# VectorE turns x in squares of 32 instead of TensorE, and the experts' scores become three products of rounded halves in 64x128 tiles

## Chip, core and metric

One core of one Trainium2 chip. The time is the device time of one execution in microseconds; for a kernel it is the median of its runs. Nothing here crosses to another core.

## What is computed

Block-sparse attention over 4 sequences of 768 tokens (8 heads of 64), whose output x, 512 wide, goes into a mixture of 4 attention experts. Cut to what matters:

```python
# attention: blocks of 32; a query block sees its neighbours, the first and last block and 3 drawn ones;
# the first and the last query block see everything
scores = np.where(mask, scale * q @ k.T, -1e9); x = softmax(scores) @ v          # x: (4, 768, 512)
logits = x @ w_gate                                   # the two best of 4 experts per token, weights w
for e in range(4):
    q, k, v = x @ wq[e], x @ wk[e], x @ wv[e]         # 64 wide
    a = softmax(np.where(causal, -1e9, 0.125 * q @ k.T))
    out += w_of_e * (a @ v @ wo[e])                   # only where e was chosen
```

The expert weights wq and wk are 64 times larger than the others, so the experts' scores need nearly full 32-bit precision.

## The kernel before, in words

**Attention.** Each sequence has 11 units of two query blocks and one "ends" unit ("g") for the first and last block. A unit gathers its keys into a tile `ks` (GpSimd copies, L620, and L300 or L298 on any of three engines), its values into `vs` (DMAs, L633 to L642), and then runs: scores on PE (mask rows L659, products L668, in 64x32 tiles), row maxima on DVE (L675, L678), exponentials on ACT (L686), four PE transposes (L697) into a PSUM bank, a copy out to `pt` (L292 on ACT or L294 on DVE), and the product with the values on PE (L714, 128x32 tiles). The ends unit does the same over all 768 keys (L760, L773, L779, L789, L802).

**x.** The product lies in a PSUM bank as queries by features. DVE multiplies it by the reciprocal row sums into an SBUF tile `x` (L731), PE transposes `x` by two 128x128 transposes into another bank (L557), ACT writes the rounded upper half `xh` (L578, L580) and DVE the remainder `xl` (L585, L587). These two halves, features by tokens, are what the experts' projections read.

**Experts.** When a chunk of tokens is done (3 tiles of 128 tokens; 4 and then 2 in the last sequence), PE projects V and the gate (L832) and Q and K for two pairs of experts (L852), each as three products of halves (`xh*wh`, `xl*wh`, `xh*wl`) in a 32-bit form that the matmul rounds. Q and K are copied out once, unrounded, to `qk` (L292 on ACT or L294 on DVE). For every row tile r of 128 queries and each pair p of experts ("a score block", 48 in all, over 128(r+1) keys): the causal mask (L934) and the scores (L943) in 64x32 tiles as full 32-bit products, which the trace shows as two MATMUL records for each instruction; maxima (L956, DVE), exponentials (L961, ACT), gate weight over row sum (L966 to L968, DVE), scaling (L975, GpSimd or DVE), transposes (L991, PE), copies to `pte` (L292, L294), the product with V (L1012, PE), halves `oh` and `ol` (L1022 ACT, L1027 DVE), output projection (L1036, PE), a copy to `y` and a store.

**Order.** All this is recorded as operations with an engine (or a choice), a duration and dependences. A table of characters, `ORDER`, found by a search outside, says in which sequence each engine gets its instructions; `replay` assigns buffers and PSUM banks from small pools along it. The engines run in their order and wait by semaphores. Changes between PE tile shapes (128x128, 128x32, 64x32) happen where neighbours in the order differ. At the start, SP, ACT and GpSimd issue the loads: K (`kt`), Q (`qt`), values, and the weights, which arrive in the still unused `qk` and `vb` tiles and are split into halves (L440, L449).

Of the kernel before, what the change touches and what calls it, by code (L numbers as in the profile page):

```python
# [25 lines left out]
ORDER = (
    "#$#&#,#2#)$W$N$P$S#/#5#;%U$]$Y$k%N$;$A%V$>$D$`#c$o&s%P$l%Y%]&3&u$u'##?#u$r&5%`%c%f$x%l%o%i&>%x%r&9)O*4'&(k&A${%/"
    "%#%,$d$J%u%2%{&;')%&'8'5#D%5',&D';(l&#%*%>&&#g%8%;&y'Y&P&G&S%A'?#x&{&V$G'V&J']'G&Y&M'`(u&]'c&`'/'r'u(x&c'3'f&)'i"
    "%D({'A'D&,)/),)#(p&f&/'J(,$#'x'l)2&i%G(r#B#H,<#o%J(/)T*5)P(D'{#8,>$)(2)Y*>(G(J#i)5)>)])`)&)))c&l)l)o(##J(')8);(Y"
    ")f*s*A#r'o)i)V$g*#)A*9'M'P$&'S&o#{)r*D)u*;)D(;)G*P)J)x){*&(N#l+X(P(5#]#`#P*S()*)*G*V*u+Y#S-f(S*,(8*/#V(?(V*J(A#M"  # L30
    '(]#Y*Z-l(`+c(c(f+f+i*M+#+&.&+)-i.)+8+,+l+u+x-{.#-`*x*{02-o+5.8-d/5-r5W.;/80;/>05+//;+2-u/A.,.>+;,G-x.A.D08*]*`/D'
    '+G*c.G,{-#,J/K/H$3,B,D+].K+o0>.2,M+>$,5J9i5P5H5N6G6J5c.5,]/M$5,Y,P.0.N*f.P+r/Q.T+A+D.`.i+J.l.c0`,S+M+{0i.f.o.s0c'
    '.v-&-)+`*i,V,`,#*l,c+P-,,f.V,i+S0A*o.x,l-/0l0f.{1;.Y/],o-27l0G->,&-A-5,)/S-8-D0D.]0o1>,,/f,/0s/`-P-H5j5T5f0v0P,r'
    ",2/i-;/c,5,u-J/#-M,8,x6S-S-V-Y/&1A1D-]0x$81V1#/l/V/)6V7-0{1G1'/Y1K5o0J0M6Y6i/o/s$/1M0S6f1P1]1`;l/u9l5l5r5u5x1iFP"
    '7/7o6N735Z1Z1S6)6]6&1o2x1m3&1x2{3)1r1{3#1c1u6,1f2#3,2&68;o322)3//,1)2A/y//6/2D2J780V/{2G7;2M0Y0#0&5{6l1,7x1/0]7>'
    '7A7M6o2,226$9e2/7J356`386c62652P262W7{6;3P9f:N2S755]7r/27u6P5a3S3Y8#8&8/823A123V3;16:I:J853?893D3]424;3G4>45483J'
    '2`2Y0)4A0,:P0/3`2^2c4f4D3M4H4o4r9o4i282;2>9r4l2f8)7D4P9u9x4J6r6u2i8-3g8A2l3d4M:&4S8;7H6x6{4V9{4Y:)3i3o3m:#3r7#3u'
    '8>8S:87&3y7)8D8l8V:S8o3{4u<P4x4|8Q:,4#:/4&7]:V2o7P8G:28Y4]:58J8M:;:Y6>:i:]:f5#7T2r:x5&8]8c5/5)4`4c8`7V7Y8g526A6D'
    '5,7`9&9>9)7c558i2u={187f9A:l:`9,9J:>9D:p:c9G9N:r:u:A:{958r8x;#8v<S;2FcFM:D9P9/8{;,;/;&;)>f7i93999;9#>`9S9V9Y9]9`'
    ';x>d;{=v>i>Y>^>{>u>l>o?#58<#</<&<2;8>y?2?;?5;;?&<)>r?8?>?A<-;>;A;J=5=8=x?,;M?/<5<85;?E?H?J?*?Y?c?f?]AYA]?`<]A,;P'  # L40
    '?iAc?MA`AfA/;]4)A2;S>#A5A8;r;5<`;D;GFBFJ;u4->&FGFE?lGAGD?p;V;Y?r>)<c<o<r<u<f<i@/?v;`=&<y<V<Y=A@8<m>,>8>/>;?P<;@;'
    '@2=D@5>>;c5>>2?SAi?VA;AB=G=J;f;i<A=SA><><{=V=#AD<DAG<G=Y=f=)>6=;4/=>>B5A=,AJ<J=/J^GMANF_=]<MGP>D>G=M=P>JB5?xAP=`'
    '=cJ`H&H)KGFSAmF`GSAo?{B8=2@#>M@>ASGV>P@&=i=lG`@BGc=oFi>S@VFf>VAVAx=rGfFl@YBP@`@]@c@fFoFrArBVFVGGGJAvA{@)G#@mBSF{'
    'Gi@EBY5D@GBA@KCr@M@j@o@P@sBDC{@SCuB;B#@uB>KACxBiH2D#BGBrBlH5BuGYBJBMBoD&G]B&BxG2C$B]FuB`HfHiD)B{FyBcC,BgH8H;HGG&'
    "@xHDC;G)@{HrC>CAB)CDCGC&A#HuN/H-G,G/C)C/CJCQCNA'JdG5HxH{I)DJI,D/KJD,CSDMDSC2DPDVD3CWGlCYD;DYD^E,HVA)H/GoC]GrC5C`"
    'E5C8GuD>I/E/D5B,CcCfI3E8E2GxE;E`EcEiB/D`D8HJH>HADAHPHMEfKDE>HSEA@,HmHoJfDiEDFZEHDDElDoDcEJEMG{CiIKI;DgDmEoDrH#HY'
    "EPESJiClDGJlIMJoJrDuIfEVIiL&ErIPEvK#J{ISKMK2KPI#ExEYI&E]IVH]F)F#E{IZKSH`HcF'I5I8DxKVKYIlI]KcK`KfF,F/I>D{IaIcIoF2"
    'K&JuF5K*KiJxI{J#LfK]KlKoJ&IAE#IrJ8L,L/CoIDIuJ;K,K/IxJME&JDJ>JAIGK5J)LiG8JHG;LrJ/KrJ,J3KuN2L)MQE)B2F8LuLxKxK{JJJ5'
    'K8OYJPNqNrL#G>L2K;F;K>JSLlLoJVL{M,O`JYL5OdM#N6OSOoOWMLMMWEW?L8LGOsL;M&M)O]OfM/M3OuW<WB]AN8MVMYLDOiOxP,P5P8Q)P/Q,'
    'P2Q/LJP&L>P)LAN;OlP;P?Q2M5M8Q5M]PBN>M`NAMiLMQ8M;PDO{M>P$PHR&MlQ;Q>NMNPNDPSR)PVP]R,QAMAP`PYQPNGR/NJQSLV]DWMMDQDR2'  # L50
    'McLPLSPJMgN{NSWGMSPMN`PcWKPfNuNxLYPPMGPjQYWWPlMoNVO#MsNYPoQVPrN]RSO&PuWYW^W`PxQ]O5O)O2R]R5NcL]M{Q`P{Q#L`R`RVR<Qf'
    'O8ODO,NfMuMxX{F>Y&XAO;WcR8NiRYX;X>N#LcQdN&N)O/NlWfN,Q&S/XDO>S2WiWuQGOARcOGY#XGOJWlQJRDS5OMYaOPRfRiWxXJXMW{XY]|SV'
    'X$SYR>S;RlS9X]XPRpS>RBRGSAS]WoWsXlSDY,Y/SGS`T5T8QMX,RrSJY2T;Y5QiRuT>TATDY>YASPSTRxRJSMQlRMR{ScTlS#RPX`SfSlSoSiS&'
    'TGYcTJTMXdToTrTPX&QoQrX)SrTuTxSuSyQuS*S{XST#X/TSXV[WTVYlYoYrZ#V&V/V2YuT&T*QxV)T{U$YDV,TYT,Q{Z&T/T]YHY)R#YfYiUDV5'
    "U'T`V<U)V8UMT2U,S,Z)Z,VJUPUG]=]>WQV>U/VDXfXiU5U2UJU8VBVHZ5VNXoY8Y;[YUSVYV]V`Vc[cUYWT[fVfU;UVU]YxUcXrYP[i[u[lViY|"
# [1037 lines left out]
```

## Time and profile before

| | |
|---|---|
| Runs | 486.59, 488.38, 489.38 us; median 488.38 |
| Profiled execution | 486.6 us, of which the span of the profile is 484.8 us; mean granted clock 0.996 |
| ACT busy | 287.6 us |
| POOL busy | 171.9 us |
| Moved by DMA | 60.87 MB, mean 126 GB/s |

The profile covers one execution. A page of it gives busy time by engine, the span in 40 slices, the chain of waits (the work that ended last, followed back from the end) and groups of instructions; the timeline lists PE's instructions by start. Matmuls are pipelined: a record's length includes the way through the array, so what a matmul costs is the distance from its start to the next start. "PE bk L852" is PE work of line 852 that writes PSUM (`bk`).

### The profile page before, as it was taken

The page shows a single profiled execution, that of the slowest core. Times are in us where ns is not written, and L with a number is a line of the kernel's source. Part 1 is how long each engine was busy: PE and PEld are TensorE (multiplying, and loading weights), DVE is VectorE, ACT ScalarE, POOL GpSimd, SP SyncE. Part 2 cuts the span into 40 slices and gives each one's busy share as a digit, 9 for nine tenths or more (in the row PEclk, how much of TensorE's full clock was granted, in tenths as well). Part 3 has the DMA queues.
Part 4 walks back from the last instruction along what each step waited for, and adds up shares of the span by engine and source line. Part 5 has one row for each costly group of instructions (what it writes and reads, how often), then busy time and mean ns, then how long its engine had stood idle before and what let it go on. Part 6 is the DMA issues. An engine that isn't in the chain of part 4 may idle for free.

```text
span 484.8 us, 24898 instructions
## 1 busy us (share of the span) xinstructions
PE 458.8 (95%) x10068; PEld 364.3 (75%) x10068; DVE 340.5 (70%) x951; ACT 287.6 (59%) x907; POOL 171.9 (35%) x464
## 2 busy tenths in 40 slices
PE   3877998999999999999999999999999999999996
...
GB/s 231 232 273 218 145 223 84 125 74 114 168 67 178 90 99 214 132 164 56 103 151 145 101 188 242 131 163 40 3 70 229 157 84 144 22 25 3 23 24 88
DMA packets 37756, 60.87 MB, mean 126 GB/s; under 512 B 9817, under 2 KB 16074, under 8 KB 37642
## 3 DMA queue, kind: packets, MB, share of 16 engines
...
## 4 chain that ended last, share of the span: by engine, by line
PE 86%; DMA 4%; issue 3%; DVE 3%; SPq 3%; ACT 2%; DVEq 0%; ACTq 0%
PE bk L852 14%; PE bk L714 8%; PE bk L943 8%; PE bk L1012 8%; PE bk L697 8%; PE bk L991 8%; PE bk L832 7%; PE bk L668 7%; PE bk L1036 6%; PE bk L557 2%; PE bk L802 2%; PE bk L789 2%; PE bk L760 2%; DMA vs<-in_v_dram 2%; SPq L642 2%
## 5 line engine op out<-in xcount | busy, mean ns | idle before, releaser
L686 ACT ACTIVATE p<-bk,mx 128x256 f32<-128x256 f32 x176 | 82.3, 483 | 26.5 <-DVE mx L678 21.8
L975 POOL TENSOR_SCALAR pe<-pe,mxe 128x640 f32<-128x640 f32 (+5 forms) x49 | 35.4, 728 | 147.8 <-DVE mxe L968 93.8
L961 ACT ACTIVATE pe<-bk,mxe 128x640 f32<-128x640 f32 (+5 forms) x96 | 60.7, 636 | 40.9 <-DVE mxe L956 40.3
L620 POOL COPY ks<-kt 128x128 f32 x264 | 65.0, 296 | 17.0 <-PE bk L668 16.9
L956 DVE TENSOR_REDUCE mxe<-bk 128x1 f32<-128x384 f32 (+5 forms) x96 | 56.2, 616 | 19.3 <-PE bk L943 18.8
L675 DVE TENSOR_REDUCE mx<-bk 128x4 f32<-128x1024 f32 x44 | 53.5, 1217 | 14.8 <-PE bk L668 14.8
L714 PE MATMUL bk<-vs,pt 128*32 128x64 f32 x2816 | 51.8, 221 | 4.1 <-DMA vs<-in_v_dram 2.5
L292 ACT ACTIVATE pte<-bk 128x512 f32<-128x512 f32 (+2 forms) x73 | 39.3, 552 | 26.7 <-PE bk L991 18.6
L714 PEld LDWEIGHTS bk<-vs,pt 128*32 128x32 f32 x2816 | 43.7, 110 | 14.7 <-issue 6.6
L668 PE MATMUL bk<-ks,qt 64*32 64x256 f32 x1408 | 50.3, 387 | 3.5 <-DMA qt<-in_qT_dram 3.5
L697 PE MATMUL bk<-ident,p 128*128 128x128 f32 x352 | 52.8, 279 | 0.4 <-DVE pte L294 0.3
L300 POOL COPY ks<-kt 128x256 f32<-128x256 f32 x40 | 15.0, 407 | 98.8 <-PE bk L668 85.7
L991 PE MATMUL bk<-ident,pe 128*128 128x128 f32 x336 | 49.9, 278 | 0.0
L943 PE MATMUL bk<-qk 64*32 64x512 f32 (+3 forms) x1024 | 47.2, 447 | 0.6 <-issue 0.6
L697 PEld LDWEIGHTS bk<-ident,p 128*128 128x128 f32 x352 | 39.3, 141 | 10.8 <-issue 3.1
L852 PE MATMUL bk<-xh,wqkh 128*128 128x384 f32 (+2 forms) x128 | 45.2, 353 | 0.0
L294 DVE COPY pte<-bk 128x512 f32<-128x512 f32 (+2 forms) x55 | 31.0, 575 | 19.9 <-PE bk L991 12.3
L1012 PE MATMUL bk<-pte,vb 128*32 128x128 f32 x1344 | 44.4, 275 | 0.5 <-issue 0.3
L991 PEld LDWEIGHTS bk<-ident,pe 128*128 128x128 f32 x336 | 37.6, 141 | 9.1 <-issue 3.3
L852 PE MATMUL bk<-xh,wqkl 128*128 128x384 f32 (+2 forms) x128 | 43.0, 336 | 0.0
L852 PE MATMUL bk<-xl,wqkh 128*128 128x384 f32 (+2 forms) x128 | 43.0, 336 | 0.0
L1012 PEld LDWEIGHTS bk<-pte,vb 128*32 128x32 f32 x1344 | 35.0, 110 | 8.6 <-issue 5.7
...
## 6 DMA issues: line engine op xcount, KB each, us to landing
...
```

The source lines that it names most:

```text
L620: pol.tensor_copy(K[:, :, k0:k0 + 32], KT[:, :, bass.ds(rv[c * NR + k] * 32, 32)])
L668: pe.matmul(Sb[32 * c:32 * c + 32, e, j * 256:(j + 1) * 256], QT[m, 2 * hh + j, q0:q0 + 32], KS[ks.i][m, 2 * hh + j, 128 * blk:128 * blk + ...
L675: vec.tensor_reduce(MX[mx.i][:, 0].rearrange("p (j e) -> p e j", e=2), BK[:, bs.i:bs.i + 2].rearrange("p e (j k) -> p e j k", j=2), AX.X, ...
L686: acte.activation(P[p.i][:, e, j], BK[:, bs.i + e, j * 256:(j + 1) * 256], AF.Exp, scale=scale, bias=MX[mx.i][:, 0, i:i + 1], accum_out=MX ...
L697: pe.transpose(BK[:, bt.i, c:c + 128], P[p.i][:, e, j, h * 128:(h + 1) * 128], ident)
L714: pe.matmul(BK[32 * c:32 * c + 32, bo.i, (2 * j + e) * 64:(2 * j + e) * 64 + 64], PT[pt.i][:, j, h, 32 * c:32 * c + 32], VS[vs.i][:, blk + ...
L852: pe.matmul(BK[:, bk.i, 0:n1 - n0], w[:, k, m0:m0 + 128], a[:, k, n0:n1], start=n_ == 0, stop=n_ == 3 * KT_ - 1)
L943: pe.matmul(BK[32 * c:32 * c + 32, banks[e].i + c0 // 512, 0:cw], QE[p][m, q0:q0 + 32], KE[p][m, c0:c0 + cw], start=c0 + cw < nk, stop=Tru ...
L956: vec.tensor_reduce(MXE[mx.i][:, 0, e:e + 1], bank(), AX.X, op=ALU.max, negate=True)
L961: acte.activation(PE_[pb.i][:, e, 0:nk], bank(), AF.Exp, bias=MXE[mx.i][:, 0, e:e + 1], accum_out=MXE[mx.i][:, 1, e:e + 1])
L991: pe.transpose(BK[:, bt.i, i * 128:(i + 1) * 128], PE_[pb.i][:, e, t * 128:(t + 1) * 128], ident)
L1012: pe.matmul(BK[32 * c:32 * c + 32, bo.i, 0:128], VB[:, t, c0:c0 + 32], PTE[ptb.i][:, e, t * 128:(t + 1) * 128], start=t == 0, stop=t == r, ...
```

## The change

Seven parts.

1. **x turned by VectorE.** The heads are laid out so that a 32-wide strip of the bank holds one pair of heads. DVE writes the scaled product back into the other half of the same PSUM bank and turns it in 32x32 squares into the first half; the two PE transposes and the tile `x` are gone. Features then lie in another order on the partitions, and the weights are loaded to match (`(p k)` instead of `(h p j)`).
2. **Experts' scores from halves.** Q and K are split at the copy out: ACT writes a rounded upper half and DVE the remainder (`QHL`, two buffers, and `KHL`). The score block is then three products, each with two instructions in 64x128 tiles, one per expert of the pair. The mask is four instructions of 64 columns instead of eight.
3. **Weights at the start.** wq and wk arrive in two of the three `pe` buffers, as packets of 1024 bytes instead of 512, one DMA each; wv is one DMA instead of two; all of them go through SP (`loadq`).
4. Unit masks are built for two blocks in one tile (`dup`), one mask instruction per 32-query strip as before (two for units at the edge).
5. The last sequence's chunks are 3 and 3 tiles, as the others' were.
6. Pools: `vs` 4 instead of 5 buffers.
7. The recording's numbers and the table `ORDER` are new.

The diff, cut to its core:

```diff
-MODEL = dict(... loadq="POOL|SP", wrel=18.0)
+MODEL = dict(... loadq="SP", xt=340, dma0=2000, wrel=18.0)
 ORDER = (
-    "#$#&#,#2#)$W$N$P$S#/#5#;%U$]$Y$k%N$;$A%V$>$D$`#c$o&s%P$l%Y%]&3&u$u'##?#u$r&5%`%c%f$x%l%o%i&>%x%r&9)O*4'&(k&A${%/"
+    '#,#2#&##$K$M$D$G$S#/#A#>$V$2#5&$$g#)$8#;$i%B#J$Y$b$5%H%J$;$c$l$o%D&&%M%P#D&`&c(P&/&2$r$u%#%&$x${$P&*%)%-%/%2%5(S'
...
-    pools = dict(ks=3, vs=5, p=2, pt=4, mx=4, x=2, pe=3, pte=2, mxe=4, oh=2, y=2)
+    pools = dict(qe=2, ks=3, vs=4, p=2, pt=4, mx=4, pe=3, pte=2, mxe=4, oh=2, y=2)
-    QK = fixed("qk", [128, 2 * EP, S])
+    KHL = fixed("khl", [128, 2, EP, S], F32R)
+    QHL = [fixed(f"qhl{i}", [128, 2, S // 2], F32R) for i in range(pools["qe"])]
...
+        wb = [buf("pe", 12 + 0.2 * i) for i in range(2)]
+            def fn(q, i=i):
+                q.dma_start(XWQ(i).rearrange("p e k d -> p e (k d)"), (wq, wk)[i].rearrange("e (p k) d -> p e (k d)", k=KT_))
+            lq.append(dma(fn, DM, 1024, eng=MODEL["loadq"], vt=12 + 0.2 * i, rel=WREL + 4 * i, new=[wb[i]], name="wq"))
...
-        def tr(o):
-            for jj in range(2):
-                pe.transpose(BK[:, bk.i, jj * 128:(jj + 1) * 128], X[x.i][:, jj * 128:(jj + 1) * 128], ident)
-        t = op("PE", 217, tr, deps, vt, "full", [bk], [x], ni=4, name=f"xt{b},{u}")
...
-            r = MX[mx.i][:, 1, :, None, None].to_broadcast([128, 4, D // 2, 2])
-            vec.tensor_tensor(X[x.i].rearrange("p (j a d) -> p a d j", j=2, a=4),
-                              BK[:, bo.i, 0:256].rearrange("p (a d j) -> p a d j", a=4, j=2), r, op=ALU.mult)
+            r = MX[mx.i][:, 1, :, None, None].to_broadcast([128, 4, D // 4, 4])
+            vec.tensor_tensor(BK[:, bo.i, 256:512].rearrange("p (k a d) -> p a d k", k=4, a=4),
+                              BK[:, bo.i, 0:256].rearrange("p (a d k) -> p a d k", a=4, k=4), r, op=ALU.mult)
+            vec.transpose(BK[:, bo.i, 0:256], BK[:, bo.i, 256:512])
...
-    CHQ = lambda b: ((0, 3), (3, 6)) if b < B - 1 else ((0, 4), (4, 6))
+    CHQ = lambda b: ((0, 3), (3, 6))
...
-                    def ev(o, bk=bk, p=p, i=i, n0=n0, n1=n1):
-                        evac(o, (QE, KE)[i][p][:, n0:n1], BK[:, bk.i, 0:n1 - n0])
+                    def hi(o, bk=bk, n=n1 - n0, halves=halves):
+                        h_, l_ = halves()
+                        acte.activation(h_, BK[:, bk.i, 0:n], AF.Copy)
+
+                    def lo(o, bk=bk, n=n1 - n0, halves=halves):
+                        h_, l_ = halves()
+                        vec.tensor_tensor(l_, BK[:, bk.i, 0:n], f(h_), op=ALU.subtract)
...
-                    for c in range(4):
-                        q0 = r * 128 + 32 * c
-                        for e in range(2):
-                            m = slice(64 * e, 64 * e + 64)
-                            pe.matmul(BK[32 * c:32 * c + 32, banks[e].i + c0 // 512, 0:cw], QE[p][m, q0:q0 + 32],
-                                      KE[p][m, c0:c0 + cw], start=c0 + cw < nk, stop=True, tile_position=(64 * e, 32 * c),
+                    for x, y_ in ((0, 0), (1, 0), (0, 1)):
+                        for e in range(2):
                             m = slice(64 * e, 64 * e + 64)
+                            pe.matmul(BK[:, banks[e].i + c0 // 512, 0:cw], QHL[qb[p].i][m, x, rc * 128:(rc + 1) * 128],
+                                      KHL[m, y_, p, c0:c0 + cw], start=c0 + cw < nk and x == y_, stop=y_ == 1, tile_position=(64 * e, 0),
```

**Where the order shows it.** PE in the first sequence, from the end of the first value product of the ends unit, before (`ident,x` are the turns of x, `ident,p` and `ident,pe` those of the probabilities, `vs` the values):

```order
L802 MATMUL bk<-vs_64,pte_84 32x64 x12
L557 MATMUL bk<-ident,x_80 128x128 x2
L697 MATMUL bk<-ident,p_69 128x128 x4
L557 MATMUL bk<-ident,x_79 128x128 x2
L789 MATMUL bk<-ident,pe_83 128x128 x2
L714 MATMUL bk<-vs_66,pt_73 32x64 x16
```

The same place of PE now:

```order
L784 MATMUL bk<-vs_65,pte_82 32x64 x12
L696 MATMUL bk<-vs_66,pt_70 32x64 x16
L696 MATMUL bk<-vs_66,pt_71 32x64 x16
L771 MATMUL bk<-ident,pe_79 128x128 x2
L680 MATMUL bk<-ident,p_69 128x128 x4
L771 MATMUL bk<-ident,pe_78 128x128 x4
```

The turns of x are gone from PE's row, here and at all 48 places; the other work has closed up and stands in another sequence.

PE at the last score block of the program before (`one` and `neg` make the mask, `qk` holds Q and K, `vb` is V):

```order
L934 LDWEIGHTS one
L934 MATMUL bk<-neg,one 32x32
L943 MATMUL bk<-qk 32x512 x8
L943 MATMUL bk<-qk 32x256 x8
L1012 MATMUL bk<-pte_85,vb 32x128 x20
```

The same block now:

```order
L914 LDWEIGHTS one
L914 MATMUL bk<-neg,one 128x64
L921 MATMUL bk<-khl,qhl_100 128x512 x6
L921 MATMUL bk<-khl,qhl_100 128x256 x6
L989 MATMUL bk<-pte_82,vb 32x128 x20
```

Eight instructions of 32 output rows per 512 keys have become six of 128. Over the whole program, changes of tile shape (the two 128x128 forms taken as one) are 236 before and 242 now.

SP's queue at the start before (`kt` is K, `vs_64` the first unit's values, whose drawn blocks are six DMAs):

```order
L318 DMA s_118<-in_samp_dram 24x6 x2
L530 DMA kt<-in_kT_dram 128x768 x2
L486 TENSOR_LOAD sc x2
L642 REGISTER_ALU
L642 ISA
L642 DMA vs_64<-in_v_dram 32x512
```

And now:

```order
L322 DMA sreg<-in_samp_dram 1x144
L535 DMA kt<-in_kT_dram 128x768 x3
L428 DMA pe_78<-in_wk_dram 128x4x256
L428 DMA pe_79<-in_wq_dram 128x4x256
L548 DMA qt<-in_qT_dram 128x4x192
L491 TENSOR_LOAD sc x2
L622 REGISTER_ALU
L622 ISA
L622 DMA vs_64<-in_v_dram 32x512
```

wk and wq, half a megabyte each, now stand ahead of the first drawn values; before, they were spread over the first five units.

More of the change, by code (lines that the diff above doesn't have):

```diff
@@ L32 @@
[L32 to L36, printed above, removed]
@@ L124, in replay @@
             if e == "PE" and o.mode != mode:
-                t += 0 if not mode or (mode, o.mode) == ("proj", "full") else -80 if (mode, o.mode) == ("full", "proj") else M["sw"][mode]
+                t += change(mode, o.mode)
             for x in o.deps:
@@ L253, in block_sparse_then_moe @@
     MX = [fixed(f"mx{i}", [128, 2, 4]) for i in range(pools["mx"])]
-    X = [fixed(f"x{i}", [128, 256]) for i in range(pools["x"])]
     PE_ = [fixed(f"pe{i}", [128, 2, S]) for i in range(pools["pe"])]
@@ L399, in c_tri @@
             pol.memset(low[:, e, 0:e], 1.0)
-    o_tri = op("POOL", 1800, c_tri, vt=12)
+    o_tri = op("POOL", 1800, c_tri, vt=12, name="tri")
     def c_heat(o):
         for _ in range(MODEL["warm"]):
-            pe.matmul(BK[:, heat.i, 0:192], row.rearrange("p a b -> p (a b)")[:, 0:128], dup[0][:, 0:192], start=True, stop=True)
+            pe.matmul(BK[:, heat.i, 0:192], row.rearrange("p a b -> p (a b)")[:, 0:128], dup[:, 0], start=True, stop=True)
     heat = buf("ps", -50)
@@ L441, in split @@
             n = WVN if scaled is False else 512
-            h = op("ACT", act(n) + (190 if scaled is not None else 0), hi, deps, vt=vt)
+            h = op("ACT", act(n) + (190 if scaled is not None else 0), hi, deps, vt=vt, use=wb if scaled else [], name=f"h{name}{vt:.1f}")
             def lo(o):
@@ L449, in lo @@
                     vec.scalar_tensor_tensor(l_, x, s, f(h_), op0=ALU.mult, op1=ALU.subtract)
-            l = op("DVE", dve(n) + (80 if scaled is not None else 0), lo, [h], vt=vt + 0.05)
+            l = op("DVE", dve(n) + (80 if scaled is not None else 0), lo, [h], vt=vt + 0.05, use=wb if scaled else [], name=f"l{name}{vt:.1f}")
             o_w[name] += [h, l]
```

356 lines of the change are left out of this document (164 added, 192 removed).

## The prediction

> **What bounds the kernel now.** I read the page first: the busy times, the slices and the chain of waits.
>
> ```profile
> PE 458.8 (95%) x10068; PEld 364.3 (75%) x10068; DVE 340.5 (70%) x951; ACT 287.6 (59%) x907; POOL 171.9 (35%) x464
> ...
> PE   3877998999999999999999999999999999999996
> ...
> PE 86%; DMA 4%; issue 3%; DVE 3%; SPq 3%; ACT 2%; DVEq 0%; ACTq 0%
> PE bk L852 14%; PE bk L714 8%; PE bk L943 8%; PE bk L1012 8%; PE bk L697 8%; PE bk L991 8%; PE bk L832 7%; PE bk L668 7%; PE bk L1036 6%; PE bk L557 2%; PE bk L802 2%; PE bk L789 2%; PE bk L760 2%; DMA vs<-in_v_dram 2%; SPq L642 2%
> ```
>
> PE is busy for 458.8 of 484.8 us, and the chain lies on PE for 86% of the time. Of its lines, the change takes away L557 and rewrites L943. Then the stretches, and what PE waits for (columns of the first: us, then busy time of PE, PEld, DVE, ACT, POOL with counts, clock, DMA share, GB/s; of the second: us in total, times, longest):
>
> ```profile
> 0.00:20.00 20.00, 9.23 (x145) 6.89 (x146) 9.09 (x35) 6.10 (x19) 15.29 (x44) 0.91 0.84 225
> 20.00:40.00 20.00, 16.64 (x445) 11.27 (x445) 13.93 (x33) 15.29 (x54) 14.23 (x47) 1.00 0.98 262
> 40.00:60.00 20.00, 16.75 (x468) 13.80 (x466) 14.09 (x43) 13.44 (x43) 4.92 (x16) 1.00 0.74 177
> ...
> 100.00:150.00 50.00, 49.62 (x1012) 37.60 (x1010) 41.50 (x104) 31.91 (x96) 22.82 (x56) 1.00 0.37 103
> ...
> 450.00:485.00 35.00, 30.61 (x542) 23.33 (x526) 19.13 (x54) 16.79 (x41) 7.02 (x8) 1.00 0.12 46
> ```
>
> ```profile
> PE bk L405 <- DVE dup L374: 7.2, 1, 7.2
> PE bk L668 <- DMA qt<-in_qT_dram: 3.5, 1, 3.5
> PE bk L714 <- DMA vs<-in_v_dram: 2.5, 1, 2.5
> PE bk L659 <- issue: 2.4, 1, 2.4
> ```
>
> PE's idle time is 26 us: 17.4 of it in the first 60 us (60 less 9.23, 16.64 and 16.75), 4.4 in the last 35, and almost none between, where 49.62 of 50 us are busy. So in the middle every microsecond of PE work that goes comes off the end, as long as the other engines keep PE fed.
>
> **The turns of x.** What a matmul costs is the distance between starts. Here are PE's timeline rows of the last row tiles (start, length):
>
> ```profile
> 459.00 0.39 PE L1036 MATMUL bk<-wol,oh 128*128 128x512 f32 x1
> 459.23 0.40 PE L1036 MATMUL bk<-woh,ol 128*128 128x512 f32 x1
> 459.55 0.23 PE L934 MATMUL bk<-neg,one 64*32 64x128 bf16 x8
> 459.61 1.28 PE L943 MATMUL bk<-qk 64*32 64x512 f32 x32
> 460.82 1.08 PE L1012 MATMUL bk<-pte,vb 128*32 128x128 f32 x32
> ...
> 463.14 2.40 PE L991 MATMUL bk<-ident,pe 128*128 128x128 f32 x20
> 465.30 0.48 PE L1036 MATMUL bk<-woh,oh 128*128 128x512 f32 x1
> ...
> 466.78 0.38 PE L991 MATMUL bk<-ident,pe 128*128 128x128 f32 x2
> 467.09 0.23 PE L934 MATMUL bk<-neg,one 64*32 64x128 bf16 x8
> 467.14 1.49 PE L943 MATMUL bk<-qk 64*32 64x512 f32 x32
> 468.57 1.63 PE L1012 MATMUL bk<-pte,vb 128*32 128x128 f32 x52
> ```
>
> Twenty transposes of this size take 465.30 - 463.14 = 2.16 us, 0.108 each. The change removes 96 (two for each of 48 units): 96 x 0.108 = 10.4 us of PE, in the packed part. With a change of tile shape after it a pair takes 0.31 us (466.78 to 467.09) instead of 0.22, so 0.09 is the price of such a change. By the order there are 242 changes instead of 236: +0.5 us.
>
> **The experts' scores.** The block that starts at 459.55 is over 640 keys and holds PE for 1.27 us (to 460.82), the one at 467.09 over 768 keys for 1.48: 0.21 us for 128 keys, 1.64 ns a key, and 0.22 us that don't depend on the keys. The new form streams the keys three times through two tiles at once. A streamed column of the 32-bit form that rounds costs 0.23 us / 512 = 0.45 ns (459.00 to 459.23), so 1.35 ns a key if the tiles of the two experts run side by side. The 48 blocks have 4 x 2 x 128 x (1+2+3+4+5+6) = 21,504 keys: 21,504 x (1.64 - 1.35) = 6.2 us less. That they run side by side is what the old form shows of its eight tiles:
>
> ```profile
> L943 PE MATMUL bk<-qk 64*32 64x512 f32 x384 | 25.9, 595 | 0.0
> ...
> L832 PE MATMUL bk<-wvl,xh 128*128 128x260 f32 x96 | 27.1, 282 | 0.0
> L832 PEld LDWEIGHTS bk<-wvl,xh 128*128 128x128 f32 x96 | 18.2, 189 | 0.0
> L943 PEld LDWEIGHTS bk<-qk 64*32 64x32 f32 x1024 | 16.7, 105 | 10.3 <-issue 8.5
> ```
>
> 384 records of 0.595 us fill 25.9 us, so about nine are in flight. No row shows a 64x128 tile. Bounds: at best 1.23 ns a key (three quarters of the 1.64, three passes for four), 2.6 us more gain; at worst one tile after the other, a rival below. The mask has four instructions of 64 columns instead of eight of 32 to 128; its eight are issued within 0.05 us now (467.09 to 467.14), so I take nothing, within 2 us over all blocks.
>
> **VectorE, ScalarE.** DVE gets 48 square turns and 32 remainders, and loses 15 plain copies of Q and K and, by the order, 17 copies of keys. The rows:
>
> ```profile
> L731 DVE TENSOR_TENSOR x<-bk,mx 128x256 f32<-128x256 f32 x48 | 29.6, 620 | 13.8 <-PE bk L714 9.1 <-PE bk L802 4.0
> L294 DVE COPY pte<-bk 128x256 f32<-128x256 f32 x19 | 8.0, 420 | 5.8 <-PE bk L789 2.9 <-PE bk L991 2.1 <-ACT p L686 0.8
> L300 DVE COPY ks<-kt 128x256 f32<-128x256 f32 x30 | 8.2, 320 | 2.3 <-DMA kt<-in_kT_dram 2.3
> L294 DVE COPY qk<-bk 128x384 f32<-128x384 f32 x9 | 5.0, 553 | 5.0 <-PE bk L852 5.0
> L961 ACT ACTIVATE pe<-bk,mxe 128x640 f32<-128x640 f32 (+5 forms) x96 | 60.7, 636 | 40.9 <-DVE mxe L956 40.3
> ```
>
> No row shows a square turn. It moves 256 columns from PSUM, as the copy of 0.42 us does; the ends are 0.32 (a copy between SBUF tiles) and 0.62 (the strided product L731). I take 0.42, the same shape from the same memory: 48 x 0.42 = 20.2 (15.4 to 29.8). The product that now writes PSUM stays at 0.62. The remainders, 384 wide, at the copy's 0.553: 17.7. Off: 15 x 0.55 = 8.3 and 17 x 0.32 = 5.4. Net +24.2 us: DVE goes from 340.5 to about 365 of 469, 78%. In its densest stretch (100 to 150, 41.5 of 50) its share of the addition is 2.5, and the stretch shrinks by 3%: 44 of 48.4, 91%. That still fits under PE, so I cost it at nothing. The cover is PE's queue of other work; if it is gone, ACT's exponentials show it first: they stand behind the turns in DVE's order by way of the maxima, and already wait 40.3 us for L956. ACT rounds all 32 upper halves where it made 17 of the copies: 15 more, some 8 us at DVE's 0.55, on an engine at 59%. The path of one unit's x loses a visit to PE's queue and gains 0.42 us. The two `QHL` buffers add a wait of ACT (chunk 1's halves for chunk 0's score blocks), but in PE's new order all six score blocks of chunk 0 stand ahead of chunk 1's Q and K projections, so nothing gets queued behind it.
>
> **Start and end.** At the start, SP now issues wk and wq, 1.05 MB, ahead of the first drawn values, which PE awaited last time at 36.7:
>
> ```profile
> 2.04 7.28 DMA kt<-in_kT_dram
> 28.73 7.88 DMA vs<-in_v_dram
> ```
>
> At the 225 GB/s of the first 20 us that is 4.7 us later for those values; but the same bytes no longer come between units 1 and 5, the near values move from SP to GpSimd's queue, and wv and wq come in fewer DMAs. The first 60 us move the same volume at a DMA share of 0.74 to 0.98. I take 0, with +5 (the whole delay on PE) and -4 (most of the 3.5 and 2.5 us of waits gone). One buffer of `vs` less and the end with chunks of 3 and 3: PE's waits for values sum to the 2.5 above, and of the 4.4 us of idleness in the last 35 the final store makes most:
>
> ```profile
> 480.45 0.40 PE L1036 MATMUL bk<-woh,ol 128*128 128x512 f32 x1
> ```
>
> From this last matmul's end to the span's end are 4.0 us, which stay. I take 0 for both, within 2.
>
> **The sum**, on the profiled execution: 484.8 - 10.4 - 6.2 + 0.5 = 468.7 us of span; with the 1.8 us around it (486.6 - 484.8) 470.5, so **471 us**. That execution is the fastest of the three, 0.4% under their median of 488.38; I leave the forecast on it. Its own range is 463 to 477: start -4, the best tile rate -2.6 and mask -2 against +5 and +2, not all at once.
>
> **The rivals.**
>
> *A. VectorE paces the dense stretches.* For it: the 91% above, 93% if a turn costs 0.62, and ACT's 40.3 us of waits for the maxima as they are. Against: at 83% (41.5 of 50) DVE leaves PE 0.4 us of idleness in that stretch, so it would have to turn from harmless to binding within a tenth. If in half of the span the 17 us can't be cashed, 8 us come back: 479.
>
> *B. The weights of the 64x128 tiles lie bare.* Every instruction of a score block needs 128 columns of new weights, against 32 before. If PE can't load them while it streams, each of 192 pairs (64 pieces of up to 512 keys, three products) adds 0.084 (189 - 105 ns) to 0.12 us: +16 to +23, the time 487 to 494. This rival ends slower, and it decides from 10.4 + 6.2 - 0.5 = 16.1 us, or 0.084 us a pair. Against it stand the L832 rows, loads of 0.189 us and matmuls with 0.0 idle, and two of these in the timeline:
>
> ```profile
> 449.42 0.28 PE L832 MATMUL bk<-wvl,xh 128*128 128x260 f32 x1
> 449.54 0.28 PE L832 MATMUL bk<-wvh,xl 128*128 128x260 f32 x1
> ```
>
> They start 0.12 us apart with new weights each, less than a load lasts, so loads run under matmuls. The Trainium skill, in "TensorE: Matmul & The Clock Gate", Part 3: Packing small matmuls, states that a weight load overlaps matmuls in flight only when its row group is another one, which here would leave half of every load bare. By that rule L832, whose loads and matmuls all use the same 128 rows, should stall, and the trace doesn't show it; no row shows the case of two row groups in use. So a small chance.
>
> *C. The two tiles run one after the other.* Then a key costs 2.70 ns: 21,504 x (2.70 - 1.64) = +22.8 us, 470.5 + 6.2 + 22.8 = 499.5. The point is 2.1 ns a key. Against: nine records in flight at L943, in both row halves.
>
> *D. The start loses 5 us* with little else wrong: 476, inside the range.
>
> *E. The PE work goes, but its time comes back as PE's waits* (the change does less than it says), because the projections await x's longer DVE path: half of 10.4 back, 476; inside too.
>
> **Chances.** Forecast with D and E, 463 to 477: 0.70. A: 0.14. B: 0.06. C: 0.05. Better than 463, by waits of the start that a new order removes: 0.05. The range 461 to 483 holds the forecast and A, and leaves out B, C and a little of the rest, under 2 in 10. A measurement of this kernel can tell about 0.5%, 2.4 us. Faster by more: 0.70 + 0.14 + 0.05 less a little of A's tail, 0.88. Within 0.5% (486 to 491): the nearer half of B and A's tail, 0.04. Slower: the rest of B and C, 0.08.
>
> **What would show it.** L557's rows gone and no idle of PE in their place; the L921 blocks at 1.2 to 1.3 us from the first mask to the next operation at 768 keys (1.35 x 768 + 0.22 = 1.26), two L921 records started close together; STREAM_TRANSPOSE near 0.42 us; DVE near 365 us; PE's busy time near 442 and its idle time still about 26. B and C show as blocks of 1.6 us and more at 768 keys, told apart by whether pairs start together. A shows as idle time of PE put down to DVE or, through ACT, to maxima. I am wrong if PE's idle time beyond 60 us grows by over 8 us, or if a score block takes longer than before.

## The result, and the profile after

The changed kernel takes 470.63 us (median of 4 runs, 469.93 to 473.48) against 488.19 us of before in the same comparison: a ratio of 0.9653, 95% interval 0.9603 to 0.9703. The forecast was 471. The profiled execution takes 471.23 us, its span 469.5. All ratios here are of runs in one state; one run of experiment 4 (503.48 us, at a granted clock of 0.983) is left out of its ratio. That the number fits doesn't say that its terms do; the experiments below show that two of them were off and that a third, which the sum didn't have, made up for it.

The page of after, busy times and the chain of waits:

```profile
PE 445.3 (95%) x9204; PEld 366.5 (78%) x9204; DVE 350.1 (75%) x974; ACT 295.2 (63%) x928; POOL 183.4 (39%) x496
...
PE 82%; DVE 8%; ACT 4%; DMA 3%; issue 2%; SPq 0%; ACTq 0%; DVEq 0%
```

PE is busy for 13.5 us less (445.3 against 458.8; the forecast said 442) and idle for 24.2 instead of 26.0: its work went and, by this view, no idleness took its place. DVE is at 350, not at 365. The chain lies on DVE for 8% instead of 3%. The stretches (us, then busy PE, PEld, DVE, ACT, POOL):

```profile
0.00:20.00 20.00, 9.06 (x188) 5.98 (x188) 8.98 (x35) 7.87 (x24) 16.30 (x49) 1.00 0.90 253
20.00:40.00 20.00, 17.23 (x480) 11.27 (x476) 18.57 (x47) 16.69 (x60) 15.95 (x49) 1.00 0.87 237
40.00:60.00 20.00, 17.07 (x460) 14.36 (x446) 13.86 (x36) 9.84 (x32) 6.32 (x22) 1.00 0.53 139
...
100.00:150.00 50.00, 50.00 (x962) 42.03 (x968) 39.04 (x104) 34.66 (x101) 14.67 (x33) 1.00 0.41 118
...
300.00:350.00 50.00, 49.55 (x978) 41.43 (x966) 41.56 (x117) 34.02 (x108) 21.14 (x56) 1.00 0.37 108
```

The start is what it was: PE is busy for 43.4 us of the first 60, before 42.6. The stretch from 100 to 150 has less DVE work than before (39.04 against 41.50), where the prediction had added to it; the densest is now the one from 300 to 350, with 41.56 of 50, as dense as the densest before and less than the 44 of 48.4 that the prediction had. PE's longest waits:

```profile
PE bk L409 <- DVE dup L385: 8.3, 1, 8.3
PE bk L784 <- issue: 2.4, 2, 1.9
PE bk L651 <- DMA qt<-in_qT_dram: 1.7, 1, 1.7
```

The wait for values is gone, that for Q is 1.7 us instead of 3.5, and the masks at the start come 1.1 us later (8.3 against 7.2). The groups of DVE that changed (count, busy us, mean ns, idle time before):

```profile
L715 DVE STREAM_TRANSPOSE bk<-bk 128x256 f32<-128x256 f32 x48 | 22.3, 465 | 1.7
L713 DVE TENSOR_TENSOR bk<-bk,mx 128x256 f32<-128x256 f32 x48 | 20.4, 426 | 7.2 <-PE bk L696 3.7 <-PE bk L784 2.5 <-ACT pte L300 0.2
L302 DVE COPY pte<-bk 128x512 f32<-128x512 f32 (+2 forms) x44 | 25.7, 597 | 8.4 <-PE bk L771 4.5 <-PE bk L968 3.0 <-ACT vb L300 0.5
```

And what ACT waits for ahead of x's upper half, by its waits, now:

```profile
ACT xh L568 <- DVE bk L715: 16.1, 14, 3.3
```

Before, on two lines:

```profile
ACT xh L580 <- PE bk L557: 16.5, 12, 3.5
ACT xh L578 <- PE bk L557: 9.5, 3, 5.8
```

A turn takes 0.465 us. The product ahead of it, L731 before, fell from 0.620 to 0.426. ACT waits for the turn for 16.1 us in all, where it waited 26.0 for PE's turn (16.5 and 9.5). The new score blocks, from the mask (L914) to the next operation's start, in PE's timeline (start, length):

```profile
436.96 0.23 PE L914 MATMUL bk<-neg,one 64*128 64x64 bf16 x4
437.03 0.94 PE L921 MATMUL bk<-khl,qhl 64*128 64x512 f32 x6
437.90 1.09 PE L968 MATMUL bk<-ident,pe 128*128 128x128 f32 x8
...
441.97 0.23 PE L914 MATMUL bk<-neg,one 64*128 64x64 bf16 x4
442.04 1.22 PE L921 MATMUL bk<-khl,qhl 64*128 64x512 f32 x12
443.19 0.66 PE L968 MATMUL bk<-ident,pe 128*128 128x128 f32 x4
...
446.05 0.26 PE L914 MATMUL bk<-neg,one 64*128 64x64 bf16 x4
446.14 1.30 PE L921 MATMUL bk<-khl,qhl 64*128 64x512 f32 x12
447.37 1.08 PE L989 MATMUL bk<-pte,vb 128*32 128x128 f32 x32
```

512 keys take 0.94 us, 640 take 1.22 and 768 take 1.32 (446.05 to 447.37). Before, 640 took 1.27 and 768 took 1.48.

### The profile page after: what moved, and what is told of

Read it like the earlier page. It is cut to its first block, busy times and chain, and to the rows that moved or that the text cites. A ratio compares the mean times of both kernels' runs of the same rounds, so it can differ in the third digit from the quotient of the medians.

```text
span 469.5 us, 23227 instructions
## 1 busy us (share of the span) xinstructions
PE 445.3 (95%) x9204; PEld 366.5 (78%) x9204; DVE 350.1 (75%) x974; ACT 295.2 (63%) x928; POOL 183.4 (39%) x496
## 3 DMA queue, kind: packets, MB, share of 16 engines
q0 software_dynamic: 5088, 15.21, 11.5%
## 4 chain that ended last, share of the span: by engine, by line
PE 82%; DVE 8%; ACT 4%; DMA 3%; issue 2%; SPq 0%; ACTq 0%; DVEq 0%
PE bk L835 12%; PE bk L696 8%; PE bk L968 8%; PE bk L651 8%; PE bk L989 8%; PE bk L680 7%; PE bk L1013 7%; PE bk L921 7%; PE bk L814 6%; PE bk L784 3%; DMA qt<-in_qT_dram 3%; PE bk L771 3%; DVE mx L658 2%; PE bk L742 2%; ACT p L669 2%
## 5 line engine op out<-in xcount | busy, mean ns | idle before, releaser
L952 POOL TENSOR_SCALAR pe<-pe,mxe 128x256 f32<-128x256 f32 (+5 forms) x58 | 39.4, 685 | 175.7 <-DVE mxe L945 71.2
L938 ACT ACTIVATE pe<-bk,mxe 128x128 f32<-128x128 f32 (+5 forms) x96 | 60.6, 636 | 31.0 <-DVE mxe L933 27.0
L933 DVE TENSOR_REDUCE mxe<-bk 128x1 f32<-128x128 f32 (+5 forms) x96 | 56.2, 616 | 13.4 <-PE bk L921 13.1
L300 ACT ACTIVATE pte<-bk 128x512 f32<-128x512 f32 (+2 forms) x84 | 42.5, 538 | 17.8 <-PE bk L968 11.0
L835 PE MATMUL bk<-xh,wqkh 128*128 128x384 f32 x128 | 44.5, 348 | 0.1
L921 PE MATMUL bk<-khl,qhl 64*128 64x512 f32 (+3 forms) x384 | 42.2, 342 | 1.0 <-issue 1.0
L835 PE MATMUL bk<-xh,wqkl 128*128 128x384 f32 x128 | 43.0, 336 | 0.0
L835 PE MATMUL bk<-xl,wqkh 128*128 128x384 f32 x128 | 43.0, 336 | 0.0
L308 POOL COPY ks<-kt 128x256 f32<-128x256 f32 x59 | 22.4, 411 | 42.3 <-PE bk L651 41.6
L300 ACT ACTIVATE pt<-bk 128x512 f32<-128x512 f32 x53 | 30.9, 607 | 10.6 <-PE bk L680 10.6
```

The costliest lines, as they stand in the source:

```text
L300: acte.activation(out_, in_, AF.Copy)
L835: pe.matmul(BK[:, bk.i, 0:n1 - n0], w[:, k, m0:m0 + 128], a[:, k, n0:n1], start=n_ == 0, stop=n_ == 3 * KT_ - 1)
L921: pe.matmul(BK[:, banks[e].i + c0 // 512, 0:cw], QHL[qb[p].i][m, x, rc * 128:(rc + 1) * 128], KHL[m, y_, p, c0:c0 + cw], start=c0 + cw < n ...
L938: acte.activation(PE_[pb.i][:, e, 0:nk], bank(), AF.Exp, bias=MXE[mx.i][:, 0, e:e + 1], accum_out=MXE[mx.i][:, 1, e:e + 1])
```

## The experiments

Ratios are to the kernel before, timed on the same chip; a hundredth is 4.9 us.

**1. What the scores are worth.** The old score block in the kernel after:

```diff
-                    for x, y_ in ((0, 0), (1, 0), (0, 1)):
-                        for e in range(2):
-                            pe.matmul(BK[:, ...], QHL[qb[p].i][m, x, rc * 128:(rc + 1) * 128], KHL[m, y_, p, c0:c0 + cw], ...)
+                    for c in range(4):
+                        for e in range(2):
+                            pe.matmul(BK[32 * c:32 * c + 32, ...], QHL[qb[p].i][m, 0, q0:q0 + 32], KHL[m, 0, p, c0:c0 + cw], ...)
-                        vec.tensor_tensor(l_, BK[:, bk.i, 0:n], f(h_), op=ALU.subtract)
```

> The kernel after, with only the score block put back to the old form: full 32-bit products in 64x32 tiles and the old mask of eight instructions; Q and K are copied out unrounded by ScalarE and VectorE leaves out the 32 remainders (17.7 us of its work). The order stays the new one. By the prediction's sum the scores' change is worth 6.2 us, so 476.8. My theory from the two traces is that pieces of 128 and 256 keys cost 0.29 and 0.45 us for six matmuls where streaming alone makes 0.17 and 0.35, so that only 2 to 6 us were gained: 473 to 477. Rival B in full (every load of weights bare) would make the old form 16 to 23 us cheaper: 448 to 455. If VectorE paces (rival A), the 17.7 us less on it give 8 us back: 463 to 469.

Measured: 474.59 us, ratio 0.9735 (0.9693 to 0.9777), against 0.9642 (0.9596 to 0.9687) of the kernel after in the run below. So the scores bring some 4 us (3.5 by the medians) where 6.2 were forecast; the two intervals leave 1.5 to 7.5, and rule out minus 16. Where the rest of the 6.2 stayed shows in PE's timeline of this kernel:

```profile
435.97 0.23 PE L923 MATMUL bk<-neg,one 64*32 64x128 bf16 x8
436.03 1.06 PE L932 MATMUL bk<-khl,qhl 64*32 64x512 f32 x16
436.90 0.22 PE L923 MATMUL bk<-neg,one 64*32 64x96 bf16 x8
...
442.21 0.23 PE L923 MATMUL bk<-neg,one 64*32 64x128 bf16 x8
442.26 1.06 PE L932 MATMUL bk<-khl,qhl 64*32 64x512 f32 x16
443.26 1.09 PE L979 MATMUL bk<-ident,pe 128*128 128x128 f32 x8
...
447.34 0.23 PE L923 MATMUL bk<-neg,one 64*32 64x128 bf16 x8
447.39 1.28 PE L932 MATMUL bk<-khl,qhl 64*32 64x512 f32 x32
448.60 0.65 PE L979 MATMUL bk<-ident,pe 128*128 128x128 f32 x4
...
451.46 0.25 PE L923 MATMUL bk<-neg,one 64*32 64x128 bf16 x8
451.52 1.52 PE L932 MATMUL bk<-khl,qhl 64*32 64x512 f32 x32
452.98 1.08 PE L1000 MATMUL bk<-pte,vb 128*32 128x128 f32 x32
```

With 768 keys the old block takes 1.52 here and the new one 1.32; with 640 it is 1.26 against 1.22, with 512 it is 1.05 against 0.94 (0.93 where the next block follows without a change of tile shape), and with 128, by the starts in both traces, 0.41 against 0.53. The gain of 0.29 ns a key, taken from the two longest blocks, doesn't hold for the shorter ones. The traces also give the sum: over all 48 blocks, from each first mask to the start of the next operation and without the gaps that the trace shows as idle, PE's row holds 45.4 us here, and 42.3 and 42.0 in the two traces of the kernel after. So the scores take 3.0 to 3.4 us off PE's row.

**2. Is PE the bound, from the new side.** One more transpose behind each four of a unit, which writes once more what was just written:

```diff
                     for h in range(2):
                         c = (2 * j + h) * 128
                         pe.transpose(BK[:, bt.i, c:c + 128], P[p.i][:, e, j, h * 128:(h + 1) * 128], ident)
+                pe.transpose(BK[:, bt.i, 384:512], P[p.i][:, e, 1, 128:256], ident)
```

> The kernel after, with 96 more 128x128 transposes on PE (two for each unit: they write once more values that PE has just written, so the result is the same), beside the unit's own, so that no change of tile shape is added. If PE is the bound and a transpose costs 0.108 us, +10.4: 481.0. If the time is set elsewhere (VectorE or ScalarE, rival A), less than 4 us: under 475. If the removed turns were worth more than their slots, as the 12.9 us between starts of the removed line and the next say, the rest lies in the visits and their shape changes, and this run still shows 10 to 11.

Measured: 476.50 us, ratio 0.9794 (0.9743 to 0.9845). The program holds 88 more, not 96 (9292 matmuls against 9204; the ends units got none), so 9.5 us were added at 0.108 each. The time grew by 5.5 us by the medians, by some 7 by the ratios, with intervals that reach from about 4 to 10. So PE's time counts, between half and in full; this run alone doesn't say which.

**3. Does VectorE's turn cost anything.** Left out:

```diff
-            vec.transpose(BK[:, bo.i, 0:256], BK[:, bo.i, 256:512])
```

> The kernel after, with the 48 square turns left out of VectorE; the halves of x are made from the unturned product, so the experts compute with x in a wrong layout. VectorE has 22.3 us less to do. My theory, that VectorE's work lies under PE's: within 1 us of the kernel after, 469.6 to 471.6. Rival A, that it paces dense stretches: at least 4 us faster, under 466.6.

Measured: 467.38 us, ratio 0.9582 (0.9541 to 0.9623). About 3 us faster than the kernel after, between the two expectations, and with intervals that overlap a little. VectorE's 22.3 us seem not free, but cheap: 0.15 us a microsecond.

**4. How thick the cover is.** Three turns for one:

```diff
             vec.transpose(BK[:, bo.i, 0:256], BK[:, bo.i, 256:512])
+            vec.transpose(BK[:, bo.i, 256:512], BK[:, bo.i, 0:256])
+            vec.transpose(BK[:, bo.i, 0:256], BK[:, bo.i, 256:512])
```

> The kernel after, with each square turn made three times (there, back and there again; the result is the same): 44.6 us more on VectorE, 350 to 395 of 470, 84%. My theory: the cover still holds nearly everywhere, 0 to 5 us slower, 471 to 476. Rival A: at least a third of it shows, 15 us or more, over 485.

Measured: 498.99 us, ratio 1.0209 (1.0147 to 1.0272): 27 to 28 us for 44.6 us of work, far from my 0 to 5 and on the side of rival A. Busy times on the page of this kernel:

```profile
PE 450.8 (91%) x9204; PEld 367.3 (74%) x9204; DVE 391.9 (79%) x1070; ACT 296.4 (60%) x928; POOL 184.7 (37%) x496
```

And ACT's wait for the turn:

```profile
ACT xh L568 <- DVE bk L717: 39.9, 30, 4.0
```

VectorE is at 79% only, and yet PE's idle time went from 24.2 us to 45.7 (496.5 - 450.8) and ACT's wait for x from 16.1 to 39.9. PE's waits that end with VectorE sum to 22.6 us instead of 9.6, those that end with ACT to 12.6 instead of 2.8. ACT's waits for the maxima ahead of the exponentials, which rival A had named as the way, sum to 60.0 instead of 58.5. So an engine doesn't have to be full to set the time; here it does so by the path of x and by VectorE's other results that PE awaits, hardly by the exponentials. Every turn more also makes the path of x longer, and no run tells the load from the path.

**5. The kernel after again, and the pieces of the score blocks.** These four ran on one chip.

> The kernel after, unchanged, as the measure for the three kernels that run on the same chip: 470.6 within 1.5 us.

Measured: 471.05 us, ratio 0.9642 (0.9596 to 0.9687).

```diff
-                for c0 in range(0, nk, 512):
-                    cw = min(512, nk - c0)
+                for c0 in range(0, nk, w_):          # w_ = nk // nb: 320 or 384 keys where there are two banks
+                    cw = min(w_, nk - c0)
```

> The kernel after, with score blocks of 640 and 768 keys cut into two equal pieces (2 x 320, 2 x 384) instead of 512 + 128 and 512 + 256; the maxima and exponentials read the two PSUM banks in that form. The same number of instructions and streamed columns. If short pieces are set by their loads and long ones by their streams (six matmuls take 0.29 us at 128 keys, 0.45 at 256, 0.54 at 384, 0.755 at 512): 640 keys go from 1.05 to about 0.99, 768 from 1.21 to 1.08, for 8 blocks each 0.5 and 1.0 us, so 1.5 us faster, and 0.5 to 2.5 with what a read of two banks may cost elsewhere. If every column costs the same 1.35 ns a key and the loads are hidden: the same time, within 0.5.

Measured: 469.46 us, ratio 0.9624 (0.9579 to 0.9669): by the medians the 1.5 us expected, but the intervals overlap, and by the starts all 48 blocks together get only 0.5 us shorter (41.5 against 42.0 in the repeat). PE's timeline of this kernel:

```profile
438.94 0.23 PE L915 MATMUL bk<-neg,one 64*128 64x64 bf16 x4
439.01 1.12 PE L922 MATMUL bk<-khl,qhl 64*128 64x320 f32 x12
440.07 0.66 PE L969 MATMUL bk<-ident,pe 128*128 128x128 f32 x4
...
448.74 0.26 PE L915 MATMUL bk<-neg,one 64*128 64x64 bf16 x4
448.82 1.30 PE L922 MATMUL bk<-khl,qhl 64*128 64x384 f32 x12
450.06 2.39 PE L990 MATMUL bk<-pte,vb 128*32 128x128 f32 x80
```

A block of 640 keys falls from 1.22 to 1.13 us; one of 768 keeps its 1.32. So the piece of 128 keys was 0.1 us dearer than its streams, and the piece of 256 was not.

```diff
-                for c0 in range(0, nk, 512):
-                    cw = min(512, nk - c0)
+                for c0 in range(0, nk, 256):
+                    cw = min(256, nk - c0)
```

> The kernel after, with score blocks cut at every 256 keys instead of every 512: the same streamed columns, 32 pieces more, so 192 more matmuls and loads of weights. If loads run under streams, as the prediction had it: no change, within 0.5 us. If loads are partly bare in pieces of 256 keys and shorter (0.45 us for six matmuls at 256 keys, 0.755 at 512): 24 pieces of 512 cost 0.15 more each, 8 of 384 about 0.2 more, +5.2 us, 474 to 477. Rival B in full (0.187 us of load bare for each pair): 96 pairs more, +18.

Measured: 471.58 us, ratio 0.9673 (0.9635 to 0.9711). No longer than the kernel after by more than the measurement tells, and not by 5; by the starts, all 48 blocks together hold PE's row for 43.4 us instead of 42.0. Its blocks:

```profile
435.67 0.23 PE L914 MATMUL bk<-neg,one 64*128 64x64 bf16 x4
435.74 0.96 PE L921 MATMUL bk<-khl,qhl 64*128 64x256 f32 x12
436.62 1.09 PE L968 MATMUL bk<-ident,pe 128*128 128x128 f32 x8
```

512 keys take 0.95 us with twelve matmuls and as many loads, 0.94 with six. My theory that in pieces of 256 the loads lie bare is wrong: loads of 0.187 us run under streams of 256 keys, of which each pair, one for each expert, starts 0.12 us after the last.

```diff
-                    for x, y_ in ((0, 0), (1, 0), (0, 1)):
-                        for e in range(2):
+                    for e in range(2):
+                        for x, y_ in ((0, 0), (1, 0), (0, 1)):
```

> The kernel after, with the six matmuls of a piece in another order: the three products of the first expert, then the three of the second, so that neighbours in PE's row use the same 64 rows and the same PSUM bank. Streams and loads are as many. If tiles run side by side only where neighbours use different rows, as the prediction assumed: a key costs up to 2.70 ns instead of 1.35, 21,504 x 1.35 = up to 29 us slower, 485 to 500. If the neighbours' order doesn't matter: 470 to 472.

Measured: 469.56 us, ratio 0.9651 (0.9595 to 0.9708), and a block of 768 keys at 1.33 us, as before the swap:

```profile
448.28 0.26 PE L914 MATMUL bk<-neg,one 64*128 64x64 bf16 x4
448.37 1.31 PE L921 MATMUL bk<-khl,qhl 64*128 64x512 f32 x12
449.61 2.39 PE L989 MATMUL bk<-pte,vb 128*32 128x128 f32 x80
```

The order of the two experts inside a piece doesn't matter. Whether the chip got the matmuls in the written order the trace doesn't tell, since their names are alike.

**6. What the turn was worth in the old order.** Three kernels made from the one before, in its order. In the first, PE's turns are left out:

```diff
-            for jj in range(2):
-                pe.transpose(BK[:, bk.i, jj * 128:(jj + 1) * 128], X[x.i][:, jj * 128:(jj + 1) * 128], ident)
+            return
```

> The kernel before, with PE's 96 turns of x left out and nothing in their place: the halves of x are made from the unturned product in its SBUF tile, so the experts compute with x in a wrong layout. The forecast's term is 10.4 us: 477.6. By the starts in the trace of before, the turns hold PE's row for 12.9 us, with their visits: 475. If, as the spare transposes in the kernel after showed (11.7 us of PE's row, 5.5 to 6 us of time), PE's row has slack that gives and takes half of it, 481 to 483.

Measured: 480.82 us, ratio 0.9894 (0.9857 to 0.9931): 5.2 us, 3.4 to 7.0. Half of the forecast's 10.4, although PE's work is gone. (VectorE has 3.7 us more than before, 344.2 instead of 340.5, 2 us of it because the remainders now read x from SBUF: 0.462 us each instead of 0.418.) In the second, VectorE turns the old product on top of that:

```diff
+            vec.transpose(BK[:, bo.i, 0:256], X[x.i])
```

> The same, with VectorE's 48 square turns put in (from the product in SBUF into PSUM; nobody reads the result), some 20 us of VectorE: the work of the change's first part alone, in the order and with the scores of before. If that work lies under PE's, as the prediction had it: the time of the kernel without turns, within 1 us. If VectorE costs here what it does in the kernel after (3.4 us for 22.3, by leaving the turns out there): 3 to 4 us more than that kernel, 479 to 486. If the cover is as thin as the three turns showed (28 us for 44.6): 10 us more or worse.

Measured: 490.31 us, ratio 1.0087 (1.0053 to 1.0122): slower than before by 2.6 to 6.0 us. In the third, the product goes to PSUM too, so that this is the change's first part by itself, but for the turn's result, which goes to the SBUF tile `x` instead of PSUM:

```diff
-            vec.tensor_tensor(X[x.i].rearrange("p (j a d) -> p a d j", j=2, a=4), ...)
+            vec.tensor_tensor(BK[:, bo.i, 256:512].rearrange("p (k a d) -> p a d k", k=4, a=4), ...)
+            vec.transpose(X[x.i], BK[:, bo.i, 256:512])
```

> The kernel before with the change's first part alone: PE's 96 turns of x are left out, VectorE writes the scaled product into the other half of its PSUM bank (0.43 us in the kernel after, 0.62 before) and turns it in squares (0.465 us) into the tile x, from which the halves are made; order, start, scores and buffers are those of before. The weights' rows are not laid out to match, so the experts compute with x in another order of features. VectorE has some 9 us less than in the kernel with a turn and the old product (490.3), and some 13 to 15 more than in the one without any turn (480.8). If the first part makes the gain by itself, as the prediction's sum had it (10.4 us): 476 to 478. If VectorE's time has the price that those two kernels show in this order (9.5 us for 20.8): 486 to 488, no gain, and the rest of the change (new order, start, scores) makes all of the 17 us. If VectorE's price is a matter of single waits that a shorter product heals: 481 to 484.

Measured: 484.37 us, ratio 0.9924 (0.9891 to 0.9956): 3.7 us, 2.1 to 5.3. The busy times on the page of the first, without any turn:

```profile
PE 453.5 (94%) x9972; PEld 357.2 (74%) x9972; DVE 344.2 (71%) x951; ACT 287.6 (60%) x907; POOL 174.7 (36%) x464
```

Of the second, with VectorE's turn of the old product:

```profile
PE 458.0 (94%) x9972; PEld 357.6 (73%) x9972; DVE 365.0 (75%) x999; ACT 288.1 (59%) x907; POOL 174.7 (36%) x464
```

And of the third, the change's first part:

```profile
PE 453.4 (94%) x9972; PEld 355.5 (74%) x9972; DVE 355.7 (74%) x999; ACT 288.5 (60%) x907; POOL 174.7 (36%) x464
```

PE's work is the same in all three, and 10.4 us less than before. The profiled executions differ in clock: the first's was granted 0.984 of full speed and the second's 0.985, the third's 0.996 like before's, so only the third's busy time can be set beside the 458.8 of before. It is 5.4 us less, not 10.4, and PE's idle time is 26.6 us instead of 26.0. The order of PE is that of before but for the turns, so the starts in the traces can be compared step by step. In the third's, the steps that held the turns are 7.9 us shorter together and all others 3.2 us longer, while the gaps that count as idle are the same: PE's busy time holds waits. In the first's, the steps with the turns are 9.5 us shorter and the others 7.5 longer, but 5.2 of these fall in the first 60 us, in an execution 3.7 us over its median, where the clock was 0.91, 0.94 and 0.89 by stretches of 20 us (before 0.91, 1.00 and 1.00).

VectorE's first 11.5 us (344.2 to 355.7) cost some 1.5 us by the ratios, which is within what the intervals leave open, the next 9.3 (to 365.0) cost 8. The path from the product to the halves grows along with the load, from 0.62 us to 0.88 and 1.08 by the mean lengths, so the price is that of both. The second's runs also had a somewhat lower clock (0.985 to 0.993) than those of before beside them (0.986 to 0.996).

**7. The turn into SBUF**, on top of the equal pieces:

```diff
-            vec.transpose(BK[:, bo.i, 0:256], BK[:, bo.i, 256:512])
+            vec.transpose(XS[XI[b, u]], BK[:, bo.i, 256:512])        # two tiles in turn
```

> The kernel with equal score pieces, and VectorE's turn written to one of two SBUF tiles instead of PSUM; ScalarE and VectorE read x from there. If an operation with one end in PSUM is cheaper than with both, the turn falls from 0.465 us towards 0.32 to 0.42 and the remainder likewise, 2 to 9 us less on VectorE, and at the price seen for leaving the turn out (0.15 us of time for one of VectorE) 0.3 to 1.5 us faster than the kernel with equal pieces: 468 to 469. If the strided product's lesson holds (0.62 us into SBUF against 0.43 into PSUM), the turn gets dearer by some 0.2 us, 9 us in all, and the time 1 to 5 us longer: 470 to 475.

Measured: 470.31 us, ratio 0.9681 (0.9649 to 0.9713), no gain. The groups:

```profile
L573 DVE TENSOR_TENSOR xl<-xs,xh 128x256 fp32r<-128x256 f32 x48 | 22.0, 463 | 8.0 <-ACT xh L570 7.9
L718 DVE STREAM_TRANSPOSE xs<-bk 128x256 f32<-128x256 f32 x48 | 21.6, 450 | 1.7
```

The turn gets 0.015 us cheaper, and those who read x get dearer: VectorE's remainder 0.463 instead of 0.417, ScalarE's half 0.421 instead of 0.389. Neither expectation named that. No version tried that still turns x is faster than the kernel after by more than the measurement tells.

## Why the prediction was right, point by point

**The sum was right by offset, which is luck.** It had 10.4 for PE's turns, 6.2 for the scores and nothing else of weight. By the ratios, the turn's move alone brings 3.7 us (0.9924), the scores some 4 (0.9735 to 0.9642), and 9 come between the two (0.9924 to 0.9735; the intervals leave 6.6 to 11.8), from what else the change does: the new order with its choice of engines, the start, the chunks, the masks and buffers. The prediction had costed these at +0.5 for changes of shape and 0 for the rest.

**"So in the middle every microsecond of PE work that goes comes off the end" is the step that failed.** The sentence had a condition, that the other engines keep PE fed, and it is the condition that didn't hold: with 10.4 us of PE work gone, 5.2 came off (3.4 to 7.0). The stretch with 49.62 of 50 us busy was read as PE at work. But a matmul's record covers its way through the array (transposes that start 0.108 us apart have records of 0.28), so short waits between starts vanish under it. The third kernel of experiment 6 shows that at the clock of before: PE's records lost 5.4 us, not 10.4, and its idle time stayed. Which waits came back isn't shown one by one. The Trainium skill, "Perfetto Trace Analysis", Identifying the Most-Contended Engine, states that the busy share of matmuls is no good measure of how close a kernel is to its limit, because they are pipelined, and that the work done as a share of the peak and the busy share of weight loads should be read instead. In the kernel before the busy share of matmuls reads 95% and that of loads 75%; the experiments bear out that the first misleads, and don't test the second. Rival E, that part of the PE work comes back as waits, was right about the turns. It was priced well (half of 10.4) and called part of the forecast; but it was to show as PE's waits for the longer path of x, and it shows before VectorE's turn is put in.

**"That still fits under PE, so I cost it at nothing" failed too.** The cover for VectorE is real but thin. In the old order the forecast's VectorE load, 365 us, costs 9 us more than no turn at all (0.9894 to 1.0087), so the turn with the old product would have made the kernel slower. In the new order, 22 us of turns cost 3 and another 45 cost 28. Rival A was right that VectorE can pace PE at such a load; its price, 8 us, is about what the old order would have paid. Its path, by the maxima and ACT's exponentials, isn't what the runs show: from the first kernel of experiment 6 to the second ACT's waits for the maxima fall, from 77.6 us to 72.9, and with three turns they grow by 1.5 only. Rival A was set aside because PE was idle for only 0.4 us in the densest stretch: the same misreading of PE's busy time.

**VectorE's load came out at 350, not 365.** By the groups: the product is cheaper by 48 x 0.194 = 9.3, the turn dearer by 2.1 (22.3 instead of 20.2), 44 copies of `pte` instead of 55 (25.7 us instead of 31.0), and GpSimd takes more of the scaling (L975, now L952; VectorE's part falls from 20.3 to 17.8). Together 15.0. The remainders at 0.55 us and the halves on ACT were as costed.

**The scores: right in the mechanism, the term too large.** The two tiles run side by side: from 512 to 768 keys a block grows by 0.38 us (0.94 to 1.32), 1.48 ns a key, where the prediction had 1.35 and C 2.70. C is out. B is out as well: 192 more matmuls with their loads, in pieces of 256 keys, lengthen PE's row by 1.4 us, where B in full had 18. The Trainium skill's rule behind B, that a load overlaps only matmuls of another row group ("TensorE: Matmul & The Clock Gate", Part 3: Packing small matmuls), gives no price here that the runs show: with neighbours in the same 64 rows, as the code has them, the block takes 1.33 us, and with neighbours in different rows 1.32. B is right only for pieces of 128 keys, 0.1 us dearer than their streams, as the equal pieces show for blocks of 640 keys; two of six block sizes have one, 16 blocks, an estimate of 1.6 us. The step that was mis-sized is the price of the new form. The prediction's lines add up to 45.8 us for the old blocks (21,504 x 1.64 ns and 48 x 0.22 us) and 39.6 for the new (1.35 ns). By the starts, the old ones take 46.0 in the kernel before and 45.4 in experiment 1, and the new ones 42.0 to 42.3: dearer by 2.4 to 2.7 than their streams and the 0.22 us, of which the pieces of 128 keys may be 1.6.

**Start and end** are as costed: PE's work in the first 60 us differs by 0.7 us, and the waits that went (2.5 for values, 1.8 for Q) are partly taken up by the later masks.

**What stays open** is what the 9 us in the middle are. VectorE's load falls too, from 355.7 us in the third kernel of experiment 6 to 337.8 in the one with the old scores: Q's and K's copies moved to ACT, key copies moved to GpSimd (13 on VectorE instead of 30) and there are fewer copies of `pte`. But by the old order's prices that explains little: the 18 us lie below 356 us, where a microsecond of VectorE cost 0.13 (11.5 us cost 1.5), which makes some 2 us; only at the price above 356 would they pay for all of it. Nor does one kind of PE's work stand out between the two traces: counted from start to start, idle gaps left aside, the largest difference is 2.0 us for the units' value products (L713, L706). No run has the new work in the old order, and the sequence itself, the chunks of 3 and 3 and the start were not changed one by one. So more than half of the gain has no cause that is shown.
